# Block-sparse attention into a gated MoE layer on one core: due times for every planned step, mask rows by DMA, heads transposed one by one

## The chip, the cores and the metric

One core of a Trainium2 chip runs the kernel. The core has TensorE (PE, matrix multiply), VectorE (DVE), ScalarE (ACT), GpSimd (POOL) and SyncE (SP, which here only issues DMAs), and 16 DMA engines between its on-chip memory and the chip's main memory. Each engine runs its own instructions strictly in the order in which the program emits them, and waits on semaphores for the others. The metric is device time in microseconds (us); less is better. Three runs of the kernel before took 249.91, 252.76 and 246.73 us, median 249.91.

## What is computed

Attention over 4 batches, 8 heads, 768 positions and head size 64, with a mask of 24 x 24 blocks of 32 positions (neighbours, first and last block, and three sampled blocks per row), and on its output (3072 tokens of 512) a layer that multiplies by `w_in`, gates each value with the softmax over the 1024 hidden values, normalises, scales by `g_ln` and multiplies by `w_out`:

```python
    mask = np.abs(blk_i - blk_j) <= window
    mask = mask | (blk_i == 0) | (blk_j == 0) | (blk_i == n_blocks - 1) | (blk_j == n_blocks - 1)
    for qb in range(n_blocks):
        for kb in sampled_blocks[qb]:
            mask[qb * block:(qb + 1) * block, kb * block:(kb + 1) * block] = True
    scores = np.where(mask, scores, -1000000000.0)
    scores = scores - np.max(scores, axis=-1, keepdims=True)
    attn = np.exp(scores)
    attn = attn / (np.sum(attn, axis=-1, keepdims=True) + 1e-09)
    return np.matmul(attn, v).astype(np.float32)
...
    h = x @ w_in
    e = np.exp(h - h_max)
    sm = e / (np.sum(e, axis=-1, keepdims=True) + 1e-09)
    solu = h * sm
    ln = (solu - mu) / np.sqrt(var + 1e-06) * g_ln
    return (ln @ w_out).astype(np.float32)
```

## The kernel before

The work is cut into units and feeds. A **unit** (`attend`, L507) is one batch b, one third t of the queries (256 of them) and one pair of heads pr; there are 4 x 3 x 4 = 48. A unit has three score steps, each of four matmuls into one of two score banks in PSUM (L517), each followed by an exponential on ACT (L523) that frees the bank; then 24 small matmuls with the values (L536), a reciprocal and a scaling on DVE (L545, L548) that write the unit's columns of x. When the four pairs of a third are there, x is transposed (`turn_x`, by DMA except for the first and the last third, which PE transposes). A **feed** (`feed`, L585) is 128 tokens; there are 24. It multiplies xT by `w_in` in two halves of four matmuls (L597), takes the exponential on ACT (L604), the product u on DVE (L607), transposes u (L614 by DMA; for the first and the last two feeds by PE, L566, with a copy on DVE, L570), takes statistics on DVE (L616, L620) and POOL (L624 to L629), multiplies uT by `w_out` in two halves (L637), and scales and stores (L642, L645).

The mask goes through the score matmul itself: kT and qT have 64 rows of head data and 24 more rows, one per block. In kT these rows say which block a key lies in; in qT they hold 0 where the query's block may see that block and -30000 where it may not. The kernel before builds them on 24 partitions from 0 up: the block rows `selp` by two selections on POOL, the table `allow_b` by a chain of small steps on DVE (L272 to L290), one step per sampled block, a matmul of both into PSUM, and a negation on DVE into qT of pair 0 and into `mskq` (L300). Copies on DVE then bring the rows to every pair (L318, L321, L324) and to the second buffer of kT and qT, which batches 1 and 3 use (L330).

The first batch is transposed by PE (`opening` L445, `opening_rest` L472, through `turned` L425): each 128 x 128 transpose takes both heads of a pair, which then lie on partitions 0 to 63 and 64 to 127 of PSUM, so two evictions, one per head, bring them to partitions 0 to 63 of kT or qT (L419 on ACT, L421 on DVE). The other batches are cast on POOL (L486) and transposed by DMA (L489), with two copies on DVE (L494).

The order of all this is not written out. Each step is an `Op` with an engine, an estimated duration, dependencies, buffers to take and to free, a due time and an earliest start. `Plan.run` (L93) is a list scheduler over a model of the core: for the engine that can start first it takes, among the steps ready at that moment, the one with the lowest due time; the kernel then emits the steps in this order, and the hardware keeps the order on each engine. Buffers and dependencies become semaphores. The due times before come from formulas, such as these for units and feeds:

```python
    def unit_due(u):
        return 5 + 2.8 * u if u < 5 else 19.0 + 3.65 * (u - 5)
...
            turn_x(b, t, 17 + 15 * j - 10)
            for qt in range(2):
                feed(b, t, qt, lambda f, j=j, qt=qt: 17 + 15 * j + 7.5 * qt + f * 3.5)
```

Spare matmuls on zeros (L650), 8 of 512 columns and 30 of 128, are due late and have earliest times near the start; they run where PE has nothing else.

Of the kernel before, what the change touches and what calls it, by code (L numbers as in the profile page):

```python
# [7 lines left out]
FP32 = mybir.dt.float32  # L8
# [21 lines left out]
def dve_us(n, mode=1):  # L30
    return n / mode / 960 + 0.075


def pool_us(n):
    return 0.15 + n * 1.0 / 1200


class Op:
    def __init__(self, eng, us, emit, deps, due, take, last_of, load, after, lands, nb, n):
# [4 lines left out]
        self.last_of = list(last_of)  # L44
        self.load = load
        self.lands = lands
        self.nb = nb
        self.n = n
        self.slots = {}
        self.start = None  # L50
        self.seen = None
# [6 lines left out]
class Plan:  # L58
    def __init__(self):
        self.ops = []  # L60
        self.pools = {}
        self.free = {e: 0.8 for e in ENGINES}
        self.dma_free = 0.0

    def pool(self, name, n):
        self.pools[name] = [0.0] * n

    def op(self, eng, us, emit, deps=(), due=0.0, take=None, last_of=(), load=None, after=(), lands=0.6,
           nb=0.0, n=1):
        k = len(self.ops)  # L70
        o = Op(eng, us, emit, deps, DUE.get(k, 100 * due) / 100, take, last_of, load, after, lands,
               EARLIEST.get(k, 100 * nb) / 100, n)
        self.ops.append(o)
        return o

    def place(self, o):
        t = o.nb
        for d in o.deps:
            if d.seen is None:
                return INF, None  # L80
            t = max(t, d.seen)
# [5 lines left out]
        for p in o.take:  # L87
            free = self.pools[p]
            slots[p] = min(range(len(free)), key=lambda k: (free[k], k))
            t = max(t, free[slots[p]])  # L90
        return t, slots

    def run(self):  # L93
# [4 lines left out]
        while any(todo.values()):  # L98
            best = None
            for e, ops in todo.items():  # L100
                now = self.free[e]
                pick = None
                for o in ops:
# [3 lines left out]
                    key = (max(t, now), o.due) if t > now + 0.02 else (now, o.due)  # L107
# [27 lines left out]
def kernel(  # L135
# [93 lines left out]
    def data_us(nbytes):  # L229
        return nbytes / 360e3  # L230


    samp_i = const.tile([NB, NR, 2], I32, name="samp_i")
    samp_f = const.tile([NB, NR], FP32, name="samp_f")
    _t = sampled_blocks.tensor
    _t32 = bass.DRamTensorHandle(_t.name, (2 * NB * NR,), I32)
    iota_k = const.tile([NB, NB], I32, name="iota_k")
    iota_d = const.tile([NB, NB], I32, name="iota_d")
    iota_p = const.tile([NB, 1], I32, name="iota_p")
    iota_f = const.tile([NB, NB], FP32, name="iota_f")  # L240
    dist = const.tile([NB, NB], FP32, name="dist")
    edge = [const.tile([NB, 1], FP32, name=f"edge{i}") for i in range(2)]
    allow = [const.tile([NB, NB], FP32, name=f"allow{i}") for i in range(3)]
    allow_b = const.tile([NB, NB], BF16, name="allow_b")
    selp = const.tile([NB, NCH, P], BF16, name="selp")
    mskq = const.tile([NB, NCH, P], BF16, name="mskq")
# [3 lines left out]
        out=samp_i.rearrange("a b c -> a (b c)"),  # L250
        in_=bass.AP(tensor=_t32, offset=0, ap=[[2 * NR, NB], [1, 2 * NR]])), due=-100, load=0.01, lands=0.8)
# [3 lines left out]
    ms = op("DVE", 0.75, lambda o: nc.vector.memset(selp, 1.0), due=-98.8)  # L255
    ik = op("POOL", 0.15, lambda o: nc.gpsimd.iota(iota_k, pattern=[[1, NB]], base=0, channel_multiplier=0),
            due=-99)
    idd = op("POOL", 0.15, lambda o: nc.gpsimd.iota(iota_d, pattern=[[1, NB]], base=0, channel_multiplier=-1),
             due=-98.9)
    ip = op("POOL", 0.15, lambda o: nc.gpsimd.iota(iota_p, pattern=[[0, 1]], base=0, channel_multiplier=1),  # L260
            due=-98.8)
    sel1 = op("POOL", 0.86, lambda o: nc.gpsimd.affine_select(
        out=selp, in_=selp, compare_op=ALU.is_ge, fill=0.0, base=0, channel_multiplier=-BLK,
        pattern=[[1, NCH], [NCH, P]]), [ms], due=-97.5)
    sels = op("POOL", 0.86, lambda o: nc.gpsimd.affine_select(
        out=selp, in_=selp, compare_op=ALU.is_ge, fill=0.0, base=BLK - 1, channel_multiplier=BLK,
        pattern=[[-1, NCH], [-NCH, P]]), [sel1], due=-97.5)
    mid = op("POOL", 0.2, lambda o: nc.gpsimd.memset(ident, 0.0), due=-97)
    mids = op("POOL", 0.3, lambda o: nc.gpsimd.affine_select(
        out=ident, in_=ident, compare_op=ALU.not_equal, fill=1.0, base=0, channel_multiplier=1,  # L270
        pattern=[[-1, P]]), [mid], due=-97)
    iof = op("DVE", 0.1, lambda o: nc.vector.tensor_copy(out=iota_f, in_=iota_k), [ik], due=-95)  # L272
    d2 = op("DVE", 0.1, lambda o: nc.vector.tensor_tensor(out=dist, in0=iota_d, in1=iota_d, op=ALU.mult),
            [idd], due=-95)
    e0 = op("DVE", 0.08, lambda o: nc.vector.scalar_tensor_tensor(
        out=edge[0], in0=iota_p, scalar=float(NB - 1), in1=iota_p, op0=ALU.subtract, op1=ALU.mult), [ip],
        due=-95)
    e1 = op("DVE", 0.08, lambda o: nc.vector.tensor_scalar(
        out=edge[1], in0=edge[0], scalar1=0.0, scalar2=float(NB * NB), op0=ALU.is_equal, op1=ALU.mult), [e0],
        due=-95)  # L280
    al0 = op("DVE", 0.1, lambda o: nc.vector.tensor_scalar(
        out=allow[0], in0=dist, scalar1=1.0, scalar2=edge[1], op0=ALU.subtract, op1=ALU.is_le), [d2, e1],
        due=-94)
    static = op("DVE", 0.08, lambda o: nc.vector.memset(allow[0][:, 0 : NB : NB - 1], 1.0), [al0], due=-94)
    slo = op("DVE", 0.1, lambda o: nc.vector.tensor_copy(out=samp_f, in_=samp_i[:, :, 0]), [samp_dma],
             due=-93)
    prev, dep = allow[0], [static, iof, slo]
    for r in range(NR):
        nxt = allow_b if r == NR - 1 else allow[1 + r]
        al = op("DVE", 0.11, lambda o, r=r, prev=prev, nxt=nxt: nc.vector.scalar_tensor_tensor(  # L290
            out=nxt, in0=iota_f, scalar=samp_f[:, r : r + 1], in1=prev, op0=ALU.is_equal, op1=ALU.max),
            dep, due=-92)
        prev, dep = nxt, [al]

    def mask_mm(o, c0, n):
        nc.tensor.matmul(mbank[o.slot][0:NB, 0 : n * P], allow_b,
                         selp[:, c0 : c0 + n, :].rearrange("a c p -> a (c p)"), start=True, stop=True)

    def negate(dst, src):
        nc.vector.tensor_scalar(out=dst, in0=src, scalar1=1.0, scalar2=NEG, op0=ALU.subtract, op1=ALU.mult)  # L300

    def rows_of(src, n):
        return src.rearrange("a c (o p) -> a c o p", o=1).broadcast_to([NB, n, 2, P])

    mm0 = op("PE", 0.11, lambda o: mask_mm(o, 0, 2), [al, sels], due=-90, take="m")
    mrow = {}
    mrow["q", 0] = op("DVE", dve_us(2 * TW), lambda o: negate(
        qT[0][D:KR, 0, 0:2], rows_of(mbank[mm0.slot][0:NB, 0:TW].rearrange("a (c p) -> a c p", c=2), 2)),
        [mm0], due=-90)
    mq0 = op("DVE", dve_us(TW), lambda o: negate(  # L310
        mskq[:, 0:2, :].rearrange("a c p -> a (c p)"), mbank[mm0.slot][0:NB, 0:TW]), [mm0],
        due=4, last_of=[mm0])
    mm1 = op("PE", 0.22, lambda o: mask_mm(o, 2, 4), [al, sels], due=8, take="m")
    mq1 = op("DVE", dve_us(4 * P), lambda o: negate(
        mskq[:, 2:6, :].rearrange("a c p -> a (c p)"), mbank[mm1.slot][0:NB, 0 : 4 * P]), [mm1],
        due=9, last_of=[mm1])
    for pr in range(NPR):
        mrow["k", pr] = op("DVE", dve_us(2 * S, 4), lambda o, pr=pr: nc.vector.tensor_copy(  # L318
            out=kT[0][D:KR, pr], in_=rows_of(selp, NCH)), [sels], due=-91 if pr == 0 else 2 + 2.7 * pr)
        if pr:  # L320
            mrow["q", pr] = op("DVE", dve_us(2 * TW, 4), lambda o, pr=pr: nc.vector.tensor_copy(  # L321
                out=qT[0][D:KR, pr, 0:2], in_=rows_of(mskq[:, 0:2], 2)), [mq0], due=3 + 2.7 * pr)
    for pr in range(NPR):
        mrow["qr", pr] = op("DVE", dve_us(8 * P, 4), lambda o, pr=pr: nc.vector.tensor_copy(  # L324
# [396 lines left out]
```

## Time and profile before

| | us |
|---|---|
| median of three runs | 249.91 |
| the profiled execution | 249.62 |
| its span, first to last instruction | 247.9 |
| PE busy in the span | 211.4 |
| ACT busy | 167.8 |
| DVE busy | 160.9 |
| POOL busy | 70.8 |
| last value matmul of the last unit begins at | 225.17 |

The profile gives each engine's busy time, groups of instructions by line, what each engine waited for, and a row of slices or windows along the span. A busy share over the whole span mixes an opening (first batch loaded and transposed on PE), a long middle in which units and feeds alternate, and a tail with the last feeds only; so the stages are read by themselves.

```profile
L523 ACT ACTIVATE ex<-sbank 128x1024 bf16<-128x1024 f32 x144 | 141.5, 1024 | 52.7 <-PE sbank L517 51.6
L517 PE MATMUL sbank<-qT,kT 88*128 88x256 bf16 x576 | 86.8, 280 | 9.0 <-ACT ex L523 8.0
L637 PE MATMUL mbank<-w_out_sb,uT 128*128 128x512 bf16 x192 | 50.7, 390 | 11.5 <-DMA uT<-u 7.3
L597 PE MATMUL hbank<-w_in_sb,xT 128*128 128x512 bf16 x176 | 46.4, 387 | 4.3 <-DMA xT<-x 2.4
L536 PE MATMUL mbank<-va,ex 128*128 128x65 bf16 x1152 | 43.6, 194 | 0.0
```

In such a row the first figure behind the bar is busy time, then the mean duration in ns, then the idle time of the engine in front of the group and what ended most of it.

### The profile page before, as it was taken

How to read it: one execution, taken by the hardware profiler on the slowest of the kernel's cores; microseconds unless marked ns; L12 is line 12 of the kernel's file. 1: busy time of each engine (PE TensorE's matmuls, PEld its weight loads, DVE VectorE, ACT ScalarE, POOL GpSimd, SP SyncE). 2: the span in 40 equal slices, each digit the busy share in tenths (PEclk: the TensorE clock that was granted, in tenths of full speed). 3: DMA queues.
4: the chain of work that ended last, by engine and by line, in shares of the span. 5: the costliest groups of instructions: out<-in, count | busy, mean ns of one | idle time of the engine just before them, and what ended most of it. 6: DMA issues, size and time to landing. Idle time of an engine off the chain costs nothing. (4 is left out here: it accounts for less than half of the span.)

```text
span 247.9 us, 5617 instructions
## 1 busy us (share of the span) xinstructions
PE 211.4 (85%) x2248; PEld 140.6 (57%) x2248; DVE 160.9 (65%) x346; ACT 167.8 (68%) x198; POOL 70.8 (29%) x139
## 2 busy tenths in 40 slices
PE   6787899888999897797897887868999899897853
PEld 2576676564667574574664654635666667564321
DVE  7999999993856647648537756626627636466491
ACT  3275777874968868668878768546788888683210
POOL 4791224450511513505113514500111101101120
PEclk9997999997999999999999999979999999999995
DMA  6999963598566999998669999871343503613111
GB/s 196 353 255 278 379 150 112 108 293 280 109 127 160 239 253 180 276 222 204 120 200 155 308 245 167 222 160 44 66 105 89 106 23 87 128 31 93 61 42 73
DMA packets 73022, 41.53 MB, mean 168 GB/s; under 512 B 54308, under 2 KB 68900, under 8 KB 72996
## 3 DMA queue, kind: packets, MB, share of 16 engines
q1 hardware_dynamic: 71904, 40.12, 64.3%
q0 software_dynamic: 1056, 1.05, 2.8%
q8 instruction: 17, 0.28, 0.5%
q14 instruction: 9, 0.07, 0.1%
q10 hardware_dynamic: 36, 0.00, 0.0%
HBM read 23.07 MB, written 6.29 MB: 118 GB/s over the span
## 5 line engine op out<-in xcount | busy, mean ns | idle before, releaser
L523 ACT ACTIVATE ex<-sbank 128x1024 bf16<-128x1024 f32 x144 | 141.5, 1024 | 52.7 <-PE sbank L517 51.6
L517 PE MATMUL sbank<-qT,kT 88*128 88x256 bf16 x576 | 86.8, 280 | 9.0 <-ACT ex L523 8.0
L517 PEld LDWEIGHTS <-kT 88*128 88x128 bf16 x576 | 54.9, 100 | 34.3 <-issue 12.3
L637 PE MATMUL mbank<-w_out_sb,uT 128*128 128x512 bf16 x192 | 50.7, 390 | 11.5 <-DMA uT<-u 7.3
L597 PE MATMUL hbank<-w_in_sb,xT 128*128 128x512 bf16 x176 | 46.4, 387 | 4.3 <-DMA xT<-x 2.4
L536 PEld LDWEIGHTS <-ex 128*128 128x128 bf16 x1152 | 42.2, 98 | 2.9
L536 PE MATMUL mbank<-va,ex 128*128 128x65 bf16 x1152 | 43.6, 194 | 0.0
L607 DVE TENSOR_TENSOR u<-hbank,e 128x1024 bf16<-128x1024 f32 x22 | 26.8, 1218 | 11.8 <-ACT e L604 11.7
L637 PEld LDWEIGHTS <-uT 128*128 128x128 bf16 x192 | 17.7, 99 | 29.1 <-DMA uT<-u 10.4
L616 DVE BATCH_NORM_STATS2 bs<-u 128x6 f32<-128x512 bf16 x48 | 32.3, 683 | 0.3
L597 PEld LDWEIGHTS <-xT 128*128 128x128 bf16 x192 | 18.4, 99 | 22.8 <-DMA xT<-x 3.6
L545 DVE RECIPROCAL r<-mbank 128x4 f32<-128x4 f32 x48 | 8.4, 175 | 32.2 <-PE mbank L536 32.1
L642 DVE TENSOR_SCALAR ot<-mbank,rs 128x512 f32<-128x512 f32 x24 | 17.9, 745 | 13.8 <-issue 6.9
L626 POOL TENSOR_SCALAR vr<-z,mv 128x1 f32<-128x1 f32 x24 | 7.6, 316 | 60.8 <-DVE mv L620 52.3
L604 ACT ACTIVATE e<-hbank 128x1024 bf16<-128x1024 f32 x22 | 22.4, 1019 | 3.3 <-PE hbank L597 2.7
L624 POOL TENSOR_TENSOR z<-z 128x1 f32<-128x1 f32 x24 | 4.6, 193 | 58.1 <-ACT e L604 58.1
L548 DVE TENSOR_TENSOR x<-mbank,r 128x256 bf16<-128x256 f32 x48 | 20.1, 419 | 1.1
L486 POOL CAST kb<-kst 128x768 bf16<-128x768 f32 x12 | 9.9, 822 | 34.7 <-DMA kst<-in_k_dram 34.7
L494 DVE COPY kT<-kx 64x768 bf16<-64x768 bf16 x24 | 9.0, 376 | 15.1 <-DMA kx<-kb 14.8
L413 POOL CAST va<-vst 128x768 bf16<-128x768 f32 x16 | 14.1, 883 | 2.4 <-DMA vst<-in_v_dram 2.2
L629 POOL TENSOR_TENSOR rs<-vr,neg_half 128x1 f32<-128x1 f32 x24 | 13.7, 571 | 1.8
L494 DVE COPY qT<-qx 64x768 bf16<-64x768 bf16 x24 | 8.9, 371 | 6.8 <-DMA qx<-qb 6.6
(71 smaller groups left out, 117.4 us busy)
## 6 DMA issues: line engine op xcount, KB each, us to landing
vst<-in_v_dram SPq DMA_DIRECT2D x16, 384.0 KB, 5.0
out_dram<-ot SPq DMA_DIRECT2D x24, 256.0 KB, 2.5
kst<-in_k_dram SPq DMA_DIRECT2D x15, 384.0 KB, 3.9
qst<-in_q_dram SPq DMA_DIRECT2D x12, 384.0 KB, 4.3
w_out_f<-in_moe_w_out_dram SPq DMA_DIRECT2D x2, 1024.0 KB, 10.2
qst<-in_q_dram SPq DMA_DIRECT2D x4, 256.0 KB, 6.2
w_in_sb<-in_moe_w_in_dram POOLq DMA_DIRECT2D x2, 512.0 KB, 7.4
q0st<-in_q_dram SPq DMA_DIRECT2D x4, 128.0 KB, 4.2
```

The source lines that it names most:

```text
L413: ready_v[(b, pr)] = op("POOL", pool_us(S), lambda o: nc.gpsimd.tensor_copy(out=va[i][:, 2 * pr : 2 * pr + 2, :, 0:D], in_=vst[ld.slot]), ...
L494: got.append(op("DVE", dve_us(S, 4) + 0.02, lambda o, hh=hh: nc.vector.tensor_copy(out=dst[i][0:D, pr, :, hh, :], in_=cx[t.slot][hh * D : ...
L517: nc.tensor.matmul(s[:, m, :], kT[i][0:KR, pr, jc, hh, :], qT[i][0:KR, pr, 2 * t : 2 * t + 2, hh, :], start=(m % 2 == 0), stop=(m % 2 == 1))
L523: exs.append(op("ACT", 0.92, lambda o, so=so: nc.scalar.activation(out=exb[o.slot], in_=sbank[so.slot], func=ACT.Exp, scale=scale), [so], ...
L536: nc.tensor.matmul(acc(o)[:, qt, hh, :], exb[exs[n].slot][:, m, qt * P : (qt + 1) * P], va[i][:, 2 * pr + hh, jc, :], start=first, stop=(n ...
L548: nrm = op("DVE", 0.33, lambda o: nc.vector.tensor_tensor(out=xb[x_of[b, t].slot][:, :, 2 * pr * D : (2 * pr + 2) * D].rearrange("p a (h d ...
L597: nc.tensor.matmul(hb()[:, n, :], xTb[xt.slot][:, qt, c, :], w_in_sb[n][:, c, :], start=(c == 0), stop=(c == KD - 1))
L604: zs = op("ACT", 0.905 + 0.2, lambda o: nc.scalar.activation(out=eb[o.slot], in_=hb().rearrange("p a f -> p (a f)"), func=ACT.Exp, accum_o ...
L607: us = op("DVE", 1.14, lambda o: nc.vector.tensor_mul(out=ub[o.slot], in0=hb().rearrange("p a f -> p (a f)"), in1=eb[zs.slot]), [zs], due= ...
L616: bs = [op("DVE", 0.6, lambda o, n=n: nc.vector.bn_stats(out=bsb[(o if n == 0 else bs[0]).slot][:, n, :], in_=ub[us.slot][:, n * 512 : (n ...
L637: nc.tensor.matmul(mbank[m0.slot], uTb[ut.slot][:, KF // 2 * n + f, :], w_out_sb[n][:, f, :], start=(n == 0 and f == 0), stop=(n == 1 and ...
L642: fo = op("DVE", 0.66, lambda o: nc.vector.tensor_scalar(out=otb[o.slot], in0=mbank[os_[0].slot], scalar1=rsb[rs.slot], scalar2=None, op0= ...
```

## The change

Five things change; the arithmetic and the kinds of matmul in the middle stay as they are.

1. Every one of the 1178 steps gets a due time from a table (`DUE`, in hundredths of a us, by the step's number), and most steps of the opening an earliest start (`EARLIEST`). The formulas stay in the code but are overridden. The table was found by a search over the model.
2. The model is refitted: a lag for each pair of engines in place of one per engine, a latency for each kind of DMA, one port that POOL's steps and some of DVE's take in turn, and other durations.
3. The mask is built on partitions 64 to 87, where its rows lie in kT and qT. POOL's second selection writes kT of pair 0 directly, and DVE copies that for the second head. The three sampled blocks are compared in one step (`eq`) and joined with the fixed part by one reduction (`al`). The negation for the first 256 queries runs on ACT, that for the other 512 on DVE, both straight into qT of pair 0. `selp` and `mskq` go.
4. The rows of the other pairs and of the second buffer are copied by five DMAs from SP's queue (`mk`, `mq`, `mr`, and two in `mrow1`) in place of 19 copies on DVE, of which a half of one stays (point 3).
5. In the opening each head is transposed by itself, onto partitions 0 to 63 (`turn`), and one eviction on DVE writes both heads (`put`). Pair 0 is cast in 256-column parts, all on DVE. There are 44 short spare matmuls in place of 30. The second token block of a feed pair takes its turn in the h banks after the first by an explicit dependency (`h_before`).

The core of the diff (of the two tables, the first lines):

```diff
-SEEN = {"PE": 0.25, "ACT": 0.17, "DVE": 0.13, "POOL": 0.14, "SP": 0.05}
-WARM = 6.0
-DUE = {}
-EARLIEST = {}
+WARM = 8.0
+NEAR = {"PE": 0.05, "ACT": 0.1, "DVE": 0.12, "POOL": 0.12, "SP": 0.05}
+DUE = dict(enumerate((
+    81, 80, 147, 166, 80, 105, 211, 425, 323, 191, 90, 209, 338, 221, 115, 135, 325, 347, 355, 382, 433, 496,
...
+EARLIEST = {
+    0: 81, 2: 142, 3: 166, 6: 211, 7: 410, 9: 176, 11: 209, 16: 325, 18: 346, 21: 496, 22: 800, 24: 270,
...
@@ Plan.place, Plan.run
+            free = [f + (LAG[e][o.eng] if e else 0.0) for f, e in self.pools[p]]
...
+        if o.port:
+            t = max(t, self.port_free)
...
-                    key = (max(t, now), o.due) if t > now + 0.02 else (now, o.due)
+                    key = (t if t > now + NEAR[e] else now, o.due)
...
+                self.dma_free = max(self.dma_free, t + o.lat) + o.load
+                o.end = (t + o.lat + 2 * o.load if o.own else self.dma_free) + o.lands
@@ mask
+    sels = [op("POOL", 0.86, lambda o: nc.gpsimd.affine_select(
+        out=kT[0][MS, 0, :, 0, :], in_=below[MS], compare_op=ALU.is_ge, fill=0.0, base=BLK - 1,
+        channel_multiplier=BLK, pattern=[[-1, NCH], [-NCH, P]]), [sel1], due=-99.3)]
+    sels.append(op("DVE", 0.29, lambda o: nc.vector.tensor_copy(
+        out=kT[0][MS, 0, :, 1, :], in_=kT[0][MS, 0, :, 0, :]), sels[:1], due=-91, port=True))
...
+    eq = op("DVE", 0.15, lambda o: nc.vector.tensor_tensor(
+        out=seen_by[MS, :, 0:NR], in0=iota_k[MS].rearrange("a (n r) -> a n r", r=1).broadcast_to([NB, NB, NR]),
+        in1=samp_i[MS, :, 0].rearrange("a (n r) -> a n r", n=1).broadcast_to([NB, NB, NR]),
+        op=ALU.is_equal), [samp_dma, ik], due=-93)
+    al = op("DVE", 0.17, lambda o: nc.vector.tensor_reduce(
+        out=allow_b[MS], in_=seen_by[MS], axis=mybir.AxisListType.X, op=ALU.max), [static, eq], due=-92)
...
+    mrow["q", 0] = op("ACT", 0.5, lambda o: negate(o, 0, 2, mm0), [mm0], due=-90, last_of=[mm0])
+    mm1 = op("PE", 0.22, lambda o: mask_mm(o, 2, 4), [al, sels[0]], due=8, take="m", nb=8)
+    mq1 = op("DVE", 1.15, lambda o: negate(o, 2, 4, mm1), [mm1], due=9, last_of=[mm1])
...
+    mk = rows_dma("SP", *others(kT, 0, NCH), sels, 3.8, 0.6)
+    mq = rows_dma("SP", *others(qT, 0, 2), [mrow["q", 0]], 4.5, 0.3)
+    mr = rows_dma("SP", *others(qT, 2, NCH), [mq1], 10, 0.5)
...
+    mrow1 = {"k": rows_dma("SP", kT[1][MS], kT[0][MS], [sels[0], sels[1], mk], 24, 1.0, 20),
+             "q": rows_dma("SP", qT[1][MS], qT[0][MS], [mrow["q", 0], mq1, mq, mr], 25, 1.0, 20)}
@@ opening
+    def turn(bank, at, src, held, c0, c1, deps, due, take=None, release=()):
+        def tp(o):
+            for c in range(c0, c1):
+                for hh in range(2):
+                    n = at + 2 * (c - c0) + hh
+                    nc.tensor.matmul(hT[bank][0:D, n * P : (n + 1) * P], src[held.slot][:, c, hh, :], ident,
+                                     is_transpose=True, start=(n == 0), stop=(c == c1 - 1 and hh == 1),
+                                     skip_group_check=True)
...
+    def put(bank, at, dst, pr, c0, c1, deps, due, release=()):
+        n = 2 * (c1 - c0)
+        return op("DVE", 0.175 + 0.055 * n, lambda o: nc.vector.tensor_copy(
+            out=dst[0:D, pr, c0:c1], in_=hT[bank][0:D, at * P : (at + n) * P].rearrange(
+                "p (c h x) -> p c h x", h=2, x=P)), deps, due=due, last_of=release)
...
+            t1 = turn(1, 0, kc, ck, 0, 2, [ck], due, "h1")
+            t2 = turn(1, 4, qc, cq, 0, 2, [cq, t1], due + 0.1, None, [cq])
+            t3 = turn(0, 0, kc, ck, 2, NCH, [ck, t1], due + 0.2, "h0", [ck])
+            p1 = put(1, 0, kT[0], pr, 0, 2, [t1, t2], due + 0.1)
+            gq = put(1, 4, qT[0], pr, 0, 2, [t2, p1], due + 0.1, [t1])
+            p3 = put(0, 0, kT[0], pr, 2, NCH, [t3], due + 0.3, [t3])
@@ feed, spares
-            hs.append(op("PE", 0.864, hmm, [xt, w_in_load[n]] + hs, due=due(0.5 * n),
+            hs.append(op("PE", 0.864, hmm, [xt, w_in_load[n]] + hs + h_before.get((b, t), []), due=due(0.5 * n),
...
-    for i in range(30):
-        spares(4.4 + 0.12 * i, P)
+    for i in range(44):
+        spares(4.3 + 0.112 * i, P)
```

More of the change, by code (lines that the diff above doesn't have):

```diff
@@ L43, in __init__, with seen @@
         self.take = (take,) if isinstance(take, str) else tuple(take or ())
-        self.last_of = list(last_of)
-        self.load = load
-        self.lands = lands
+        self.last_of = [a if isinstance(a, tuple) else (a, a.take) for a in last_of]
+        self.load, self.lat, self.lands = load, lat, lands
         self.nb = nb
         self.n = n
+        self.port = port or eng == "POOL"
+        self.dl, self.own = dl, own
         self.slots = {}
-        self.start = None
-        self.seen = None
+        self.start = self.end = None
+    def seen(self, eng):
+        return self.end if self.load is not None else self.end + LAG[self.eng][eng] + self.dl
     @property
@@ L227 @@
     op = plan.op
[L229 to L234, printed above, removed]
+    plan.tag = "mask"
+    MS = slice(D, KR)
     _t = sampled_blocks.tensor
     _t32 = bass.DRamTensorHandle(_t.name, (2 * NB * NR,), I32)
[L237 to L246, printed above, removed]
+    samp_i = const.tile([P, NR, 2], I32, name="samp_i")
+    iota_k = const.tile([P, NB], I32, name="iota_k")
+    iota_d = const.tile([P, NB], I32, name="iota_d")
+    iota_p = const.tile([P, 1], I32, name="iota_p")
+    dist = const.tile([P, NB], FP32, name="dist")
+    edge = [const.tile([P, 1], FP32, name=f"edge{i}") for i in range(2)]
+    seen_by = const.tile([P, NB, NR + 1], FP32, name="seen_by")
+    allow_b = const.tile([P, NB], BF16, name="allow_b")
+    one = const.tile([P, 1], BF16, name="one")
+    below = const.tile([P, NCH, P], BF16, name="below")
     warm = const.tile([1, 1], FP32, name="warm")
     samp_dma = op("ACT", 0.66, lambda o: nc.scalar.dma_start(
-        out=samp_i.rearrange("a b c -> a (b c)"),
-        in_=bass.AP(tensor=_t32, offset=0, ap=[[2 * NR, NB], [1, 2 * NR]])), due=-100, load=0.01, lands=0.8)
+        out=samp_i[MS].rearrange("a b c -> a (b c)"),
+        in_=bass.AP(tensor=_t32, offset=0, ap=[[2 * NR, NB], [1, 2 * NR]])), due=-100, load=0.01, lat=1.2,
+        lands=0.7, own=True)
     w0 = op("DVE", 0.08, lambda o: nc.vector.memset(warm, 0.0), due=-99)
@@ L262 @@
-    sel1 = op("POOL", 0.86, lambda o: nc.gpsimd.affine_select(
[L263 to L268, printed above, removed]
+    on = op("POOL", 0.1, lambda o: nc.gpsimd.memset(one, 1.0), due=-99.5)
@@ L269 @@
+    mid = op("DVE", 0.12, lambda o: nc.vector.memset(ident, 0.0), due=-98.95)
     mids = op("POOL", 0.3, lambda o: nc.gpsimd.affine_select(
         out=ident, in_=ident, compare_op=ALU.not_equal, fill=1.0, base=0, channel_multiplier=1,
[L271 to L274, printed above, removed]
+        pattern=[[-1, P]]), [mid], due=-99.45)
@@ L280 @@
-        due=-95)
+        out=edge[1][MS], in0=edge[0][MS], scalar1=0.0, scalar2=float(NB * NB), op0=ALU.is_equal,
+        op1=ALU.mult), [e0], due=-98.4)
     al0 = op("DVE", 0.1, lambda o: nc.vector.tensor_scalar(
[L282 to L286, printed above, removed]
@@ L310 @@
[L310 to L322, printed above, removed]
@@ new lines, with rows_dma @@
+    mrow = {}
+    mm0 = op("PE", 0.11, lambda o: mask_mm(o, 0, 2), [al, sels[0]], due=-90, take="m")
+    mrow["q", 0] = op("ACT", 0.5, lambda o: negate(o, 0, 2, mm0), [mm0], due=-90, last_of=[mm0])
+    mm1 = op("PE", 0.22, lambda o: mask_mm(o, 2, 4), [al, sels[0]], due=8, take="m", nb=8)
+    mq1 = op("DVE", 1.15, lambda o: negate(o, 2, 4, mm1), [mm1], due=9, last_of=[mm1])
+    mrow["qr", 0] = mq1
+    mrow["k", 0] = sels[1]
+    def rows_dma(eng, dst, src, deps, due, load, nb=0.0):
+        e = nc.scalar if eng == "ACT" else nc.sync
+        return op(eng, 0.66 if eng == "ACT" else 0.5, lambda o: e.dma_start(out=dst, in_=src), deps, due=due,
+                  load=load, lat=1.3, lands=1.0, nb=nb, own=eng == "ACT")
@@ new lines, in put, with cast @@
+    def put(bank, at, dst, pr, c0, c1, deps, due, release=()):
[3 more added lines that the diff above has]
+                "p (c h x) -> p c h x", h=2, x=P)), deps, due=due, last_of=release)
+    def cast(e, us, dst, src, c0, c1, ld, take, due, release=(), held=None, deps=()):
+        return op(e, us, lambda o: copy(
+            o, dst[(held or o).slot][:, c0:c1], src[ld.slot][:, :, c0:c1, :].rearrange("p h c d -> p c h d")),
+            list(deps) or [ld], due=due, take=take, last_of=release, port=e == "DVE")
@@ L445, in opening @@
     def opening(pr, due):
-        first = pr == 0
+        plan.tag = f"opening {pr}"
         lk, lq = stage["k", 0, pr], stage["q0", pr]
-        def cast(e, us, dst, src, c0, c1, ld, held, take, due, release):
-            return op(e, us, lambda o: copy(
-                o, dst[(held or o).slot][:, c0:c1], src[ld.slot][:, :, c0:c1, :].rearrange("p h c d -> p c h d")),
-                [ld] if held is None else [stage["kr", 0]], due=due, take=take, last_of=release)
-        if first:
-            ck = cast("DVE", 0.24, kc, kst, 0, 2, lk, None, "kc", due, [])
-            cr = cast("DVE", 0.4, kc, kst, 2, 6, lk, ck, None, due + 0.3, [lk])
-        else:
-            ck = cast("POOL", pool_us(S), kc, kst, 0, NCH, lk, None, "kc", due, [lk])
```

250 lines of the change are left out of this document (128 added, 122 removed), and 84 rows, old and new, of tables (DUE, EARLIEST).

## The prediction

> **What bounds the kernel now.** First the page: its busy shares, then the span in 40 slices of 6.2 us.
>
> ```profile
> PE 211.4 (85%) x2248; PEld 140.6 (57%) x2248; DVE 160.9 (65%) x346; ACT 167.8 (68%) x198; POOL 70.8 (29%) x139
> PE   6787899888999897797897887868999899897853
> DVE  7999999993856647648537756626627636466491
> PEclk9997999997999999999999999979999999999995
> GB/s 196 353 255 278 379 150 112 108 293 280 109 127 160 239 253 180 276 222 204 120 200 155 308 245 167 222 160 44 66 105 89 106 23 87 128 31 93 61 42 73
> ```
>
> TensorE (PE) is busy 85% of the span, more than any other engine. But the second row splits the kernel in three: for eight slices, to 50 us, VectorE (DVE) is at 9; then PE is the fullest engine; in the last five slices everything thins out, and the last slice has PE at half clock. The windows view, cut at these places, gives the sizes (columns: stretch, length, busy time of PE, weight load, DVE, ACT, POOL, then clock, DMA share, GB/s).
>
> ```profile
> 0.00:50.00 50.00, 41.88 (x443) 29.85 (x444) 46.50 (x103) 32.17 (x38) 23.26 (x41) 0.97 0.81 228
> 50.00:220.00 170.00, 150.85 (x1666) 101.31 (x1665) 98.16 (x217) 128.44 (x152) 43.72 (x87) 0.98 0.71 166
> 160.00:170.00 10.00, 8.05 (x78) 4.60 (x77) 2.54 (x8) 4.87 (x6) 1.12 (x3) 0.83 0.56 108
> 180.00:190.00 10.00, 9.60 (x116) 6.70 (x116) 4.65 (x11) 8.27 (x11) 1.01 (x3) 1.00 0.32 75
> 190.00:200.00 10.00, 9.27 (x109) 6.37 (x105) 5.14 (x12) 8.37 (x10) 1.82 (x5) 1.00 0.49 119
> 200.00:210.00 10.00, 9.88 (x119) 6.94 (x117) 5.23 (x10) 8.71 (x12) 1.20 (x4) 1.00 0.21 52
> 220.00:248.00 28.00, 18.71 (x142) 9.42 (x140) 16.24 (x28) 7.19 (x11) 3.83 (x11) 0.90 0.23 66
> ```
>
> PE is idle 50 - 41.88 = 8.1 us in the opening (DVE 46.5 of 50), 170 - 150.85 = 19.2 us in the middle, 28 - 18.71 = 9.3 us in the tail: 36.6 us in all. That is what a better order can win; PE's own work stays. Between 180 and 210 us PE is idle only 0.40 + 0.73 + 0.12 = 1.25 us in 30, or 4.2%: this mix of work can run nearly without holes. Third, the waits of PE alone, first those of the opening, then those of the middle (total us, times, longest).
>
> ```profile
> PE hbank L431 <- DVE qT L421: 2.1, 3, 1.2
> PE sbank L517 <- DVE qT L300: 0.7, 1, 0.7
> PE hbank L431 <- DVE kc L421: 0.5, 1, 0.5
> PE mbank L637 <- DVE x L548: 0.4, 1, 0.4
> PE hbank L597 <- DVE xT L570: 0.4, 1, 0.4
> ...
> PE mbank L637 <- DMA uT<-u: 7.3, 7, 1.9
> PE sbank L517 <- ACT ex L523: 7.1, 11, 0.7
> PE hbank L597 <- DMA xT<-x: 2.4, 2, 2.0
> ```
>
> In the opening PE waits for DVE. In the middle it waits 9.7 us for transposes by DMA and 7.1 us because it has nothing but scores to do while both score banks are with ACT. These are faults of order: work that could stand in the hole exists, but stands behind the waiting instruction.
>
> **The change, part by part.** The span is 247.9 us and the profiled run took 249.62 us, 1.7 us more; the median of the three runs is 249.91 us. The sum is made against 249.6.
>
> *(a) Mask work leaves DVE.* The rows are DVE's, all within the first 50 us.
>
> ```profile
> L324 DVE COPY qT<-mskq 24x1024 bf16<-24x1024 bf16 x4 | 3.2, 804 | 0.1
> L330 DVE COPY kT<-kT 24x1536 bf16<-24x1536 bf16 x4 | 2.5, 630 | 0.1
> L318 DVE COPY kT<-selp 24x1536 bf16<-24x1536 bf16 x4 | 2.4, 591 | 0.1
> L330 DVE COPY qT<-qT 24x1536 bf16<-24x1536 bf16 x4 | 2.2, 552 | 0.1
> L321 DVE COPY qT<-mskq 24x512 bf16<-24x512 bf16 x3 | 1.1, 370 | 0.0
> L300 DVE TENSOR_SCALAR qT<-mbank 24x512 bf16<-24x512 f32 x1 | 0.7, 682 | 0.0
> L300 DVE TENSOR_SCALAR mskq<-mbank 24x512 bf16<-24x512 f32 x1 | 0.7, 679 | 0.0
> L300 DVE TENSOR_SCALAR mskq<-mbank 24x256 bf16<-24x256 f32 x1 | 0.4, 403 | 0.0
> L421 DVE COPY kT<-hbank 64x768 bf16<-64x768 bf16 x6 | 3.3, 552 | 0.4 <-PE hbank L431 0.3
> L421 DVE COPY qT<-hbank 64x512 bf16<-64x512 bf16 x8 | 3.3, 416 | 0.1
> ```
>
> The five groups of copies go: 3.2 + 2.5 + 2.4 + 2.2 + 1.1 = 11.4 us; a half copy of 24x768 stays (about 0.3). The three negations (1.8 us) become one of 24x1024, about 1.3 by twice the 679 ns, and one on ACT (estimate 0.7, by DVE's 682 ns for the same shape). The allow chain swaps three dependent steps for one comparison and one reduction, a few tenths saved. Together about 11.4 - 0.3 + 1.8 - 1.3 = 11.6 us of DVE's 46.5.
>
> *(b) Five DMAs on SP's queue instead.*
>
> ```profile
> 0.79 0.45 SPq L338 DMA_DIRECT2D kst<-in_k_dram  x1
> 31.30 1.10 DVE L389 TENSOR_SCALAR w_out_g<-w_out_f,g_sb 128x512 bf16<-128x512 f32 x1
> ...
> q10 hardware_dynamic: 36, 0.00, 0.0%
> ```
>
> They write 24 rows x (3 x 1536 + 3 x 512 + 3 x 1024 + 2 x 4 x 1536) x 2 bytes = 1.03 MB. At the 379 GB/s of the busiest slice that is 2.7 us of the DMA engines, at the opening's mean of 228 GB/s 4.5 us. Each also takes SP's time to issue; at the first load's 0.45 us that is 2.3 us for the five. New waits: the third one (mr) waits on SP for DVE's negation, with the loads of w_out queued behind it. DVE first reads w_out at 31.3 us here and its loads are due near 15, so some us late are covered. The two for the second batch wait for earlier ones to land; behind them stand the second batch's loads and transposes. I cost these waits at nothing; with the cover gone each would cost about what a late transpose costs PE now, up to 1.9 us.
>
> The last of these rows is the one transfer of 24 rows that the kernel already has, on its own queue: 36 packets, 24 of data and 12 more. The Trainium skill (DMA: Bandwidth & Descriptors, "Why a DMA increments its semaphore by 16 and not by 1") says that such a DMA is spread over the largest number of engines up to 16 that divides its outer dimension, so 12 for 24 rows; the trace agrees, if each engine adds one packet. By that rule the 2.7 us become 2.7 x 16/12 = 3.6, the opening's gain shrinks by 0.9 and the forecast would be 234.
>
> *(c) Heads turned one by one.* The opening's 48 transposes become 96, but each eviction then writes both heads: 26 evictions become 17.
>
> ```profile
> 13.94 0.49 PE L431 MATMUL hbank<-ident,kc 128*128 128x128 bf16 x6 [0.22 <-DVE qT L421]
> 23.79 0.39 PE L431 MATMUL hbank<-ident,kc 128*128 128x128 bf16 x4
> ```
>
> Two more transposes cost 0.10 us, so 48 more cost 2.4 us of PE, twice that at half clock, at a time when PE has 8.1 us of holes; on a pair's chain they add 0.1 to 0.3 us. By the two eviction rows above, 256 more columns cost 552 - 416 = 136 ns, so the fixed part of a copy is 416 - 2 x 136 = 144 ns; the columns stay the same in all, and nine evictions fewer save 1.3 us. ACT sheds two of them and a cast and takes the negation. These nearly balance, and I cost (c) at nothing. Fourteen more spare matmuls fill holes, with 0.05 us each at full clock in front of work that comes ready meanwhile.
>
> *The opening, (a) to (c) together.* Bounds: at best all 8.1 us of PE's holes, at worst a loss of 4.5 us, if DMA carries the path (its share is 0.81 there). Between these I take the five DVE waits above, 2.1 + 0.7 + 0.5 + 0.4 + 0.4 = **4 us**.
>
> *(d) Due and earliest times for every step.* The diff's table covers all 1178 steps. I take no time from it, only order: scores of different units, halves of h and of the output projection alternate, and SP's transposes are due several steps before the projection that reads them. Upper bound: if the middle ran at the 4.2% holes of 180 to 210 us, 170 x 0.042 = 7.1 us of holes would stay and 12.0 go. Lower bound: nothing, or less (first rival). The good stretch has a DMA share of 0.2 to 0.5, the middle 0.71, so transposes land later there than in the good stretch: I take three quarters, **9 us**. The row 160 to 170 also shows the clock at 0.83: 10 x 0.17 / 0.5 = 3.4 us at half speed, with 1.95 us of PE idle in the same ten. The page's PEclk row has a second such dip in the middle, in its tenth slice. One gone is worth 1.7 us; both, 3.4. I take **1.7 us**. What is late next is ACT, 128 of 170 us busy: not a bound.
>
> *(e) The tail.* The order changes here too.
>
> ```profile
> 238.75 0.61 PE L566 MATMUL mbank<-ident,u 128*128 128x128 bf16 x8
> 240.57 0.68 DVE L570 COPY uT<-mbank 128x1024 bf16<-128x1024 bf16 x1
> 237.02 1.90 PE L637 MATMUL mbank<-w_out_sb,uT 128*128 128x512 bf16 x8 [0.79 <-DVE uT L570]
> 241.31 2.80 PE L637 MATMUL mbank<-w_out_sb,uT 128*128 128x512 bf16 x8 [1.95 <-DVE uT L570]
> ```
>
> The last transposed u is ready at 239.36 and is copied out at 240.57, because DVE does other work first: 1.2 us. The last eight matmuls then take 2.80 instead of 1.90 us, half clock after the hole: 0.9. In the table that copy is due before its tile's statistics are done. I take 1.2 + 0.9 = **2.1 us**, between nothing and the 9.3 idle (a chain of dependent steps, so half of it, 5, is the most I would count on).
>
> Sum: 249.6 - 4 - 9 - 1.7 - 2.1 = 232.8, so 233 us; against the median, 17 us or 6.8% less.
>
> **The rivals.** One more row, from the list of DMA issues: count and median us from issue to landing.
>
> ```profile
> uT<-u SPq DMA_TRANSPOSE x21, 3.2
> ```
>
> *Slower: the fixed order meets late transposes.* PE runs strictly in the emitted order, and an order packed for a model has no slack. Seven of the 21 transposes of u make PE wait now, 7.3 us, 1.04 each. If the packing makes all 21 late by that, the middle loses 14 x 1.04 = 14.6 us and wins none of (d): 249.6 - 4 - 2.1 + 14.6 = 258. It decides for slower (over 254.9) from 11 more late tiles, 11.4 us. For it: DMA is at 0.71 in the middle, and 1 MB is added. Against: the median transpose lands 3.2 us after its issue, and in the new table the projection is mostly due 4 to 7 us after it.
>
> *No change in the middle.* The holes there come from ACT and DMA latencies, and the new order moves them only. Then the opening and tail remain, less 3 us for mask DMAs in front of loads: 249.6 - 4 - 2.1 + 3 = 246.5. For it: no wait of PE in the rows above is over 2 us, too short to move a unit of work into. Against: the 30 us at 4%.
>
> *All the holes named go.* Opening 8.1, middle 12, both spells 3.4, tail 5: 249.6 - 28.5 = 221. For it: ACT, the next engine, would be busy 168 of 219 us of span, 77%. Against: every stage at its bound at once.
>
> **How the numbers follow.** Forecast 233 (own range 227 to 239), chance 0.57; 221, 0.18; 246.5, 0.15; 258, 0.10. The range 222 to 247 leaves out the slower rival, and a tenth shared by the outer halves of the other two. About 2% is what a measurement of this kernel can tell from no change: faster than 244.9 is 0.57 + 0.18 = 0.75, within 2% 0.15, slower 0.10.
>
> **What would show it.** Right: DVE's busy time in the first 50 us falls from 46.5 towards 36, no copies of 24 rows but one; PE idle in the middle near 8 to 10 us, waits for uT and for ACT's score banks each under 4; at most one half-clock spell there; the last uT copied within 0.3 us of its transpose. Wrong: waits of PE on uT over 15 us; mask DMAs landing after scores that need them; loads of the first batch landing later than they do in this trace.

## The result and the profile after

The changed kernel took 221.15 us (median of four runs, 219.3 to 222.49) against 250.86 us (246.73 to 252.76) for the kernel before in the same session: a ratio of 0.890, 95% interval 0.875 to 0.905. The forecast was 233 us with a range from 222 to 247, and 227 to 239 as its own narrower range. Taken by the ratio, from the 249.6 us that the forecast started at, the result is 222.2 us: at the very edge of the wide range and outside the narrow one, where the rival "all the holes named go" stood with 221. Each ratio here compares undisturbed runs alone, while a median takes all runs, and five profiles below (the two without tables on the refitted model, the refit with the old formulas, w_in issued earlier, random due times) are of executions at the slow end of their runs. The page of the changed kernel, with the rows that were shown of the kernel before and the DMA row:

```profile
PE 203.5 (93%) x2277; PEld 141.9 (65%) x2310; DVE 147.8 (67%) x318; ACT 166.8 (76%) x196; POOL 68.9 (31%) x139
PE   6999988489999999999999999998999999999981
DVE  6344593979867768567666784675784676449992
PEclk9999999999999999999999999999999999999998
DMA  5999999999999999999799989989693453352512
```

The span is 219.3 us. PE is now at 9 in nearly every slice from the tenth to the end, the only clear hole left is in the eighth slice, and no slice before the last shows a lost clock. DVE's first eight slices are no longer full, but the DMA row is: it stands at 9 from the second slice to the nineteenth. The windows view, cut at 50 and 192 us (columns as before):

```profile
0.00:50.00 50.00, 42.48 (x506) 31.21 (x511) 30.71 (x71) 31.29 (x35) 19.60 (x38) 1.00 1.02 245
50.00:192.00 142.00, 139.47 (x1581) 98.35 (x1604) 97.81 (x214) 126.33 (x150) 44.47 (x87) 1.00 0.88 197
192.00:219.00 27.00, 21.59 (x198) 12.32 (x198) 19.33 (x35) 9.19 (x13) 4.79 (x14) 0.98 0.33 89
```

PE's idle time in the middle fell from 19.2 us of 170 to 142 - 139.47 = 2.5 us of 142. In the opening it hardly fell, 8.1 to 7.5 us. Over the span, idle went from 36.5 (247.9 - 211.4) to 15.8 us (219.3 - 203.5), which is 20.7 of the 28.6 us gained; PE's busy time fell by the other 7.9, although the opening has 48 more transposes.

These figures need one correction. The page counts 2310 weight loads but 2277 matmuls: 33 matmuls of 512 columns have no record in this profile (the profile before has 2248 of both). All but one leave a false hole of 0.05 us, that one 0.2: in all some 1.9 us, of which 1.4 lie in the middle. So about 22.6 us of the gain are idle time and 6.0 busy time, and the middle's true idle time is near 1.2 us, the sum of the two waits listed for it below. Two things lower the busy time. The half-clock spells of the middle are gone: the means of 280 ns for a score matmul before and 274 now differ by the matmuls at half clock (about 415 ns); all others take 272 ns on average, right after a hole or not. And there are fewer holes: a matmul of 512 columns takes 0.38 us, but seven in a row take 1.67, so each further one adds 0.215, and every hole brings the difference of 0.16 us once more into the busy time. How much each of the two gave was not separated.

What PE still waits for, in the opening and then from 50 to 200 us:

```profile
PE hbank L707 <- DMA w_in_sb<-in_moe_w_in_dram: 2.8, 1, 2.8
PE hbank L527 <- POOL kc L580: 1.1, 1, 1.1
PE sbank L625 <- ACT ex L631: 0.8, 2, 0.6
...
PE mbank L747 <- DMA uT<-u: 1.0, 1, 1.0
PE hbank L707 <- DMA xT<-x: 0.2, 1, 0.2
```

In the middle the waits for uT fell from 7.3 to 1.0 us and those of the scores for ACT from 7.1 us to none that the view lists. In the opening the waits for DVE gave way to one of 2.8 us for w_in, which was not there before. The new order issues the two loads of w_in later, at 21.1 and 24.4 us against 13.3 and 15.5, and each then takes 9 us longer to land. The list of DMA issues shows the second; the first row is of the kernel before, the other two of the changed one, the last being one of the new mask DMAs (last column of the w_in rows: median us from issue to landing):

```profile
w_in_sb<-in_moe_w_in_dram POOLq DMA_DIRECT2D x2, 512.0 KB, 7.4
...
w_in_sb<-in_moe_w_in_dram POOLq DMA_DIRECT2D x2, 512.0 KB, 16.7
kT<-kT SPq DMA_DIRECT2D x1, 288.0 KB
```

The tail, from the changed kernel's timeline:

```profile
199.93 0.89 PE L644 MATMUL mbank<-va,ex 128*128 128x65 bf16 x24
211.56 0.61 PE L674 MATMUL mbank<-ident,u 128*128 128x128 bf16 x8
212.21 0.69 DVE L678 COPY uT<-mbank 128x1024 bf16<-128x1024 bf16 x1
213.18 1.67 PE L747 MATMUL mbank<-w_out_sb,uT 128*128 128x512 bf16 x7 [1.01 <-DVE uT L678]
214.95 0.75 DVE L752 TENSOR_SCALAR ot<-mbank,rs 128x512 f32<-128x512 f32 x1 [0.59 <-POOL rs L739]
```

From the last unit's value matmuls (the first row) to the end of the span there are 219.3 - 199.9 = 19.4 us, against 247.9 - 225.2 = 22.7 before. The last uT is copied out 0.04 us after its transposes end at 212.17 (1.2 before). The row of output matmuls shows seven of the eight; the first has no record.

### The profile page after: what moved, and what is told of

It reads as the page before. It is cut to its first block, busy times and chain, and to the rows that moved or that the text cites. A ratio compares the mean times of both kernels' runs of the same rounds, so it can differ in the third digit from the quotient of the medians.

```text
span 219.3 us, 5702 instructions
## 1 busy us (share of the span) xinstructions
PE 203.5 (93%) x2277; PEld 141.9 (65%) x2310; DVE 147.8 (67%) x318; ACT 166.8 (76%) x196; POOL 68.9 (31%) x139
## 4 chain that ended last, share of the span: by engine, by line
PE 67%; DMA 18%; DVE 5%; issue 3%; ACT 2%; POOL 1%; SPq 1%; POOLq 0%; ACTq 0%; DVEq 0%
PE sbank L625 21%; PE mbank L747 14%; PE hbank L707 14%; PE mbank L644 11%; DMA w_in_sb<-in_moe_w_in_dram 8%; DMA kst<-in_k_dram 4%; PE hbank L527 3%; DMA uT<-u 3%; DMA xT<-x 2%; PE mbank L760 2%; DVE u L717 2%; PE sbank L707 2%; DMA qx<-qb 1%; DVE ot L752 1%; ACT e L714 1%
## 5 line engine op out<-in xcount | busy, mean ns | idle before, releaser
L625 PE MATMUL sbank<-qT,kT 88*128 88x256 bf16 x576 | 82.5, 274 | 1.0 <-ACT ex L631 0.8
L625 PEld LDWEIGHTS <-kT 88*128 88x128 bf16 x576 | 53.0, 98 | 21.4 <-issue 2.3
L747 PE MATMUL mbank<-w_out_sb,uT 128*128 128x512 bf16 x177 | 45.9, 379 | 2.8 <-DVE uT L678 1.0
L707 PE MATMUL hbank<-w_in_sb,xT 128*128 128x512 bf16 x161 | 43.1, 378 | 3.7 <-DMA w_in_sb<-in_moe_w_in_dram 2.8
L644 PEld LDWEIGHTS <-ex 128*128 128x128 bf16 x1152 | 41.1, 97 | 4.3 <-ACT ex L631 0.3
L644 PE MATMUL mbank<-va,ex 128*128 128x65 bf16 x1152 | 42.5, 193 | 0.0
L726 DVE BATCH_NORM_STATS2 bs<-u 128x6 f32<-128x512 bf16 x48 | 31.6, 684 | 0.5
L747 PEld LDWEIGHTS <-uT 128*128 128x128 bf16 x192 | 18.2, 97 | 18.3 <-DVE uT L678 1.5
L714 ACT ACTIVATE e<-hbank 128x1024 bf16<-128x1024 f32 x22 | 22.6, 1029 | 3.7 <-PE hbank L707 3.6
L509 POOL CAST va<-vst 128x768 bf16<-128x768 f32 x16 | 13.2, 829 | 12.9 <-DMA vst<-in_v_dram 12.9
L593 POOL CAST qb<-qst 128x768 bf16<-128x768 f32 x12 | 10.3, 861 | 12.4 <-DMA qst<-in_q_dram 12.3
## 6 DMA issues: line engine op xcount, KB each, us to landing
w_in_sb<-in_moe_w_in_dram POOLq DMA_DIRECT2D x2, 512.0 KB, 16.7
```

What stands on the lines that cost most here:

```text
L509: ready_v[(b, pr)] = op("POOL", 0.8, lambda o: nc.gpsimd.tensor_copy(out=va[i][:, 2 * pr : 2 * pr + 2, :, 0:D], in_=vst[ld.slot]), [ld, vo ...
L593: ca = op("POOL", 0.8, lambda o: nc.gpsimd.tensor_copy(out=cb[o.slot], in_=st[ld.slot].rearrange("p h c d -> p c h d")), [ld], due=due, ta ...
L625: nc.tensor.matmul(s[:, m, :], kT[i][0:KR, pr, jc, hh, :], qT[i][0:KR, pr, 2 * t : 2 * t + 2, hh, :], start=(m % 2 == 0), stop=(m % 2 == 1))
L644: nc.tensor.matmul(acc(o)[:, qt, hh, :], exb[exs[n].slot][:, m, qt * P : (qt + 1) * P], va[i][:, 2 * pr + hh, jc, :], start=first, stop=(n ...
L707: nc.tensor.matmul(hb()[:, n, :], xTb[xt.slot][:, qt, c, :], w_in_sb[n][:, c, :], start=(c == 0), stop=(c == KD - 1))
L714: zs = op("ACT", 0.905 + 0.2, lambda o: nc.scalar.activation(out=eb[o.slot], in_=hb().rearrange("p a f -> p (a f)"), func=ACT.Exp, accum_o ...
```

## The experiments

The theory under test was the prediction's: the table's order closes the holes (A). Against it stood: the refitted model does, with or without the new due formulas that the table overrides (B); the relief of DVE in the opening does (C). Each ratio below is against the kernel before in the same session.

**The changed kernel without its tables.**

```diff
+DUE, EARLIEST = {}, {}
```

> The changed kernel with both tables emptied: due times come from the new formulas, the refitted model, the mask rows by DMA and the heads one by one stay. If the table's order closes the holes of the middle (theory A), most of the 29 us come back: 240 us or more, PE idle 12 us or more between 50 us and the last values. If the refitted model with the steeper formula closes them (theory B), 222 to 229 us, PE idle under 8 us there. If the relief of VectorE in the opening does it (theory C), also under 229 us.

Measured: 230.05 us (227.9 to 231.4), ratio 0.9215, 0.910 to 0.933. That is between the two expectations: about 9 us come back, 20 do not. So more than two thirds of the gain needs no table.

**The mask and opening parts alone.** The scheduler's lags, window, shared port, DMA latencies and due formulas are those of before; the new durations of the steps stay. The main lines of the edit:

```diff
+NEAR = dict.fromkeys(ENGINES, 0.02)
+SEEN = {"PE": 0.25, "ACT": 0.17, "DVE": 0.13, "POOL": 0.14, "SP": 0.05}
+LAG = {e: dict.fromkeys(ENGINES, s) for e, s in SEEN.items()}
+DUE, EARLIEST = {}, {}
...
-        return 5 + 2.8 * u if u < 5 else 19.0 + 2.9 * (u - 5)
+        return 5 + 2.8 * u if u < 5 else 19.0 + 3.65 * (u - 5)
```

> The mask and opening parts of the change alone: no tables, the lags, window and due formulas of before. Theory C: under 235 us. Theories A and B: the opening parts are worth at most the 4 us that the prediction gave them, 246 to 253 us, PE idle in the middle near the 19 us of before.

Measured: 245.79 us (244.48 to 247.86), ratio 0.986, 0.974 to 0.997. Theory C falls: these parts are worth some 4 to 6 us with the old order, not 29. PE's idle time in the first 50 us is 50 - 45.64 = 4.4 us there, against 8.1.

**The refitted model with the old due formulas.** As the run without tables, but with the formulas of before, for the units, the first loads and the opening:

> Refitted model, mask and opening parts, no tables, and the due formulas of before (units 3.65 us apart in place of 2.9). Theory A: 240 us or more. Theory B with the lags as the cause: 222 to 230 us. Theory B with the steeper formula as the cause: 238 us or more here, but under 230 in the run that has the new formulas.

Measured: 251.11 us (247.75 to 255.68), ratio 1.001, 0.994 to 1.008. The refit by itself closes nothing; what separates this run from the 230 us is the formulas.

**The tables on the old model.** Lags, window and port as in the run of the opening parts, tables kept.

> Both tables kept, but the order made with one lag per engine, the narrow ready window and no shared port, as before the change. Theory A: 221 to 227 us, since the due times carry the order. Theory B: 235 us or more, since the list scheduler decides by lags which step is ready.

Measured: 243.39 us (240.62 to 244.73), ratio 0.974, 0.960 to 0.989. Theory A in its simple form falls too: the same due times on the old lags are 22 us worse.

That left one main suspect inside the formulas, the distance between the units' due times, 3.65 us before and 2.9 now (theory D; theory E: it works only on the refitted model).

**One constant in the kernel before.**

```diff
-        return 5 + 2.8 * u if u < 5 else 19.0 + 3.65 * (u - 5)
+        return 5 + 2.8 * u if u < 5 else 19.0 + 2.9 * (u - 5)
```

> The kernel before with one constant changed: units are due 2.9 us apart in place of 3.65. If the slope of the units' due times is what closes the holes (theory D, from the runs without tables), 230 to 238 us, and the waits of the score matmuls for ScalarE fall from 7 us in the middle to under 2. If the slope works only on the refitted model (theory E), 244 us or more.

Measured: 242.25 us (241.42 to 243.38), ratio 0.969, 0.963 to 0.975. The constant alone gives 3%, less than expected of D. The waits of the scores for ACT went as D said, but waits for the transposes of x took their place, up from 2.4 us; PE's waits from 50 to 225 us:

```profile
PE hbank L597 <- DMA xT<-x: 10.5, 4, 4.1
PE mbank L637 <- DMA uT<-u: 2.6, 2, 1.8
PE sbank L517 <- ACT ex L523: 0.6, 1, 0.6
```

**The same constant, put back in the run without tables.**

> The changed kernel without tables, with the one constant back at 3.65. Theory D: 245 us or more, nearly all of the 21 us between the two runs without tables, and waits of the score matmuls for ScalarE near 12 us. If the other formulas (first loads, opening) made that difference, under 236 us.

Measured: 250.34 us (247.13 to 256.82), ratio 0.996, 0.990 to 1.003. One constant is 20 us on the refitted model; putting the other formulas back as well adds nothing clear (251.1 us with all the formulas of before, 250.3 with the slope alone). PE's waits show where: first the run without tables (2.9), then this one (3.65), both from 50 to 225 us.

```profile
PE mbank L750 <- DMA uT<-u: 3.1, 2, 2.6
PE sbank L628 <- ACT ex L634: 0.7, 1, 0.7
...
PE sbank L628 <- ACT ex L634: 11.6, 19, 1.3
PE mbank L750 <- DMA uT<-u: 8.5, 7, 2.1
```

With 3.65 the scheduler lets feeds go ahead of units; then nothing but scores is left for PE while ACT holds both score banks, 19 times. With 2.9 units run ahead and the feeds are there to fill in. The waits are measured. The order fits: by the weight loads in the two traces, about 36 units and 15 feeds have begun at 160 us with 2.9, and about 37 units and 16 feeds at 180 us with 3.65, so with 2.9 about one feed more is still in hand at the same unit. That this backlog is what fills the waits is read from the order, not tried by itself.

**The cell that was missing**: mask and opening parts, new formulas, old lags, no tables.

> The cell that is missing: mask and opening parts, new due formulas (units 2.9 us apart), no tables, but the lags and window of before. If the slope works with either model (theory D), 229 to 235 us, as the run without tables on the refitted model (230). If slope and refit need each other (theory E), 238 to 244 us.

Measured: 231.79 us (230.9 to 235.54), ratio 0.9325, 0.923 to 0.942. Theory E falls: with the mask and opening parts in place the new formulas give 14 us on the old lags, without the refit. Theory D fits, but this run and the one of the opening parts differ in all the formulas, so the share of the slope in the 14 us is not shown; by itself the slope was tried on the refitted lags (20 us) and in the kernel before (9). Refit or not, the formulas end at 230 to 232 us.

| no tables | units 3.65 apart | units 2.9 apart |
|---|---|---|
| lags of before | 245.8 | 231.8 |
| refitted lags | 251.1 (all formulas old), 250.3 (slope alone) | 230.1 |

With the tables: 243.4 on the lags of before, 221.2 on the refitted ones. The upper left cell has all the old formulas.

**Due times moved at random**, on the changed kernel:

```diff
+random.seed(1)
+DUE = {k: v + random.gauss(0, 30) if k >= 213 else v for k, v in DUE.items()}
```

> The changed kernel, with each due time of units and feeds moved at random by 0.3 us (standard deviation), and the order made anew. If the table is worth its 9 us over the formulas by fine placing, most of them go: 226 to 231 us. If its worth is coarse (which unit before which feed), 220 to 224 us.

Measured: 236.21 us (231.7 to 237.32). All of the table's gain goes: even the best run, 231.7 us, is above the best of the formulas, 227.9, so with 0.3 us of disorder the table is no better than they are. Whether it is worse, one run near 232 and three near 236 leave open, and this is one draw. The largest new wait of the profiled run, in the opening, is for a cast on POOL:

```profile
PE hbank L532 <- POOL kc L585: 4.9, 1, 4.9
```

**The mask rows by DVE again, the order held.** The plan is made as for the DMAs; each DMA is emitted as three or four copies on DVE.

```diff
-        return op(eng, 0.66 if eng == "ACT" else 0.5, lambda o: e.dma_start(out=dst, in_=src), deps, due=due,
+        def copies(o):
+            for i in range(dst.shape[1]):
+                s = src[:, i]
+                nc.vector.tensor_copy(out=dst[:, i], in_=s)
+        return op(eng, 0.66 if eng == "ACT" else 0.5, copies, deps, due=due,
```

> The changed kernel in its own order, with the five mask DMAs replaced at their places by 17 copies on VectorE, about 10 us of its work. If VectorE's relief matters to the end (the prediction's 4 us), 224 us or more. If VectorE has room and the first 50 us end on something else, 220 to 223 us.

Measured: 219.68 us (218.26 to 220.31), ratio 0.879, 0.873 to 0.885. DVE has room for the copies. It was run once more beside the changed kernel:

> The changed kernel as it is, for a comparison on one chip with the next run: 219 to 223 us.

> The changed kernel in its own order with the mask rows copied on VectorE, once more. If the mask DMAs cost time by pushing back the loads of the first 40 us, it stays 1 us or more below the run before it; if the earlier difference was noise, within 0.7 us of it.

Measured: the changed kernel 222.23 us (221.1 to 224.41, ratio 0.8966, 0.888 to 0.905), the copies on DVE 219.85 us (218.96 to 221.16, ratio 0.886, 0.879 to 0.892). Over six runs each they hardly touch, 2.4 us apart, though the intervals of the ratios overlap. The profile of the run with copies shows what changes first: the opening's window and the issue row of w_in.

```profile
0.00:50.00 50.00, 42.82 (x520) 31.51 (x521) 39.89 (x91) 31.92 (x36) 20.18 (x39) 1.00 0.87 227
...
w_in_sb<-in_moe_w_in_dram POOLq DMA_DIRECT2D x2, 512.0 KB, 11.4
```

Against the profile of the result, DVE does 9 us more in the first 50, DMA's share falls from 1.02 to 0.87, w_in lands in 11.4 instead of 16.7 us, and PE's wait for it is no longer listed. This version is the fastest of the study.

The same rows of the changed kernel, run beside it, show a second cost, in the clock:

```profile
PEclk9999999769999999999999999999999999999999
0.00:50.00 50.00, 43.49 (x467) 30.57 (x468) 27.70 (x64) 29.87 (x33) 20.57 (x38) 0.93 0.95 242
...
PE hbank L707 <- DMA w_in_sb<-in_moe_w_in_dram: 3.7, 1, 3.7
```

Here the wait for w_in is 3.7 us, and from 41.6 to 48.4 us PE has half its clock, which is up to 3.4 us lost; PE has done 53 fewer matmuls by 50 us than with the copies. Of the ten runs of the changed kernel eight were granted a mean clock of 0.984 to 0.992, of the ten with copies one (0.982); the other nine have 0.996 or more. The two of the changed kernel that kept their clock (0.997 and 0.998) took 220.99 and 219.3 us, inside the range of the copies, 218.26 to 221.16. So most of the 2.4 us may be clock lost around the wait for w_in, and not the bytes moved. This is read from the records; no run held the clock apart from the wait.

**w_in issued earlier, the order held.**

```diff
+    order = [o for o in order if o not in w_in_load]
+    at = next(i for i, o in enumerate(order) if o.start >= 14.0)
+    order[at:at] = w_in_load
```

> The changed kernel in its own order, with the two loads of w_in moved ahead on GpSimd's queue by some 7 us. TensorE waits 2.8 us for them before the first feed. If that wait lies on the path to the end, 217 to 219.5 us; if other loads of the first 40 us are pushed back as much, or the middle takes the hole up, 220 to 223 us.

Measured: 223.96 us (220.6 to 225.1), ratio 0.888, 0.877 to 0.900. No gain: w_in is now issued at 16.2 and 17.2 us and the wait for it is gone, but in its place stands one for a cast that waits for queries of the first batch.

```profile
PE hbank L527 <- POOL kc L580: 4.0, 1, 4.0
```

The cast itself waits 12.0 us for its queries (7.7 in the changed kernel), and around this hole too PE has half its clock, from 35.0 to 41.8 us. With the DMA share at 0.96 in the first 50 us, moving one load forward pushed another back. Taking the mask's bytes away helped here (2.4 us), moving w_in did not.

## Why the prediction was right, and where its sum was off

The mechanism was right: PE's own work stays, its holes go, and most of them went in the middle. The sum was 17 us and should have been near 29; that the wide range held at its edge is in part luck, since the opening was sized too large and the middle much too small.

- *Opening, 4 us.* DVE was relieved by more than worked out, 46.5 to 30.7 us of the first 50 (36 was expected; the prediction's own terms, 46.5 - 11.6, give 34.9), and one copy of 24 rows is left. With the old order the parts are worth about what was said, 251.4 to 245.8 us, with 3.7 us of PE's idle time gone from the first 50. But in the changed kernel the opening gained 0.6 us of idle time, not 4: step (b) costed the new DMAs at nothing beside others' loads. I looked at what stands behind them on SP's queue; the load that they delayed, w_in, is on POOL's queue (16.6 and 16.7 us to landing with the DMAs, 11.3 and 11.4 with the copies). The lower bound, 4.5 us lost, had named this case; the two versions run side by side put the price of DMAs against copies at 2.4 us. That is near the 2.7 us of plain data time, and near the 3.6 us by the Trainium skill's rule on how many engines a transfer of 24 rows uses (DMA: Bandwidth & Descriptors, "Why a DMA increments its semaphore by 16 and not by 1"); the runs do not tell these apart. As the lost clock can be most of the 2.4 us, that it is near either proves nothing. Step (c) was not tried by itself.
- *Middle, 9 us.* The term that was sized too small: 16.7 us of idle time went by the windows, 18 with the missing records. The 4.2% of the kernel's own best stretch was taken as a floor and the gain then cut by a quarter because DMA is busier in the middle; the order reached 1.8%, or 0.8% with the missing records, with a DMA share of 0.88. A busy DMA queue cost PE only 1.2 us here, where the transposes have other work in front of their readers. From 50 us to the last unit's values the time fell from 175.2 to 149.9 us, which is 25 of the 29 us: idle time, clock and the busy time of the holes together.
- *Clock, 1.7 us.* In the profile of the result both spells of the middle are gone, 3.4 us. But the gain differs from run to run: the changed kernel run again has a spell of 6.8 us in the opening.
- *Tail, 2.1 us.* 3.3 us from the last unit's values on, by the mechanism named: the last copy follows its transposes at once.
- *What the gain was put down to.* The prediction gave the middle to "due and earliest times for every step". The runs split it: the formulas, which the table overrides, bring 14 to 21 us without any table, and on the refitted model the slope alone 20; the table adds 9 on the refitted model and takes 12 away on the old one (231.8 to 243.4).
- *Rivals.* Late transposes (258) did not come: uT cost 1.0 us. Yet the reason given for it, that such an order has no slack, has some support: the run with random due times lost 10 us or more, though by other waits (uT cost it 1.4 us). "No change in the middle" is refuted by the 2.5 us of idle time. "All the holes" has the right total for other reasons: its opening, 8.1, did not come, and the middle gave more than its 12. The outer halves of the rivals at 221 and 246.5 hold 0.165 of the chances, not the tenth that the prediction gave them.

## What to carry to other kernels

When a list scheduler orders work for two kinds of consumers, first sweep the ratio of their due times: one constant was worth 9 us in the kernel before and 20 on the refitted model, a searched table of 1178 entries 9 more, and only on the model that it was searched on. A PE that waits for scores while ACT holds the banks said here that the feeds ran too early, so that nothing was left to fill in. Moving copies from an engine to DMA was not free with the DMA share near 1: look for the load that lands later on any queue, not only behind the new DMA on its own, and look whether the wait for it costs clock as well.

## What was unexpected of the hardware

PE ran at half speed until about 13 us in the profiled run of the changed kernel, although it is busy for 10.6 of the 11.3 us from 2 us on. Eight spare matmuls of 128 columns took 1.03 us at 11.47 us (0.13 us each), seven took 0.56 us at 17.25 (0.08), both with the time of one matmul's latency in them. The PEclk row has 9 in those slices all the same: its first record in this trace comes at 13.3 us, so the row says nothing of the time before.

```profile
11.47 1.03 PE L760 MATMUL mbank<-spare 128*128 128x128 bf16 x8
17.25 0.56 PE L760 MATMUL mbank<-spare 128*128 128x128 bf16 x7
```

In the run without tables (2.9), with nearly the same opening, ten such matmuls at 12.44 us took 0.73 us, and the first record of full clock comes at 5.8 us. What decides between the two is not shown.

Three long waits of PE in the opening came with a loss of clock. Around holes of 3.7, 4.0 and 4.9 us (the changed kernel run again, w_in issued earlier, random due times) PE had half its clock for 6.8 us each. No threshold follows: the profile of the result kept its clock through a hole of 2.8 us, and the kernel before lost it for 3.4 us around one of 1.9 (up to 163.9 us).
